# Row maxima sent from ScalarE's queue in an attention and mixture-of-experts kernel

## The chip, the cores and the metric

The kernel runs on one core of a Trainium2 chip. The metric is the time of one execution on the device in microseconds. The core has five engines with an instruction stream each: TensorE (PE, with its weight loads shown as PEld), VectorE (DVE), ScalarE (ACT), GpSimd (POOL) and SyncE (SP), which here does nothing but start transfers. Transfers between memories are done by 16 DMA engines that all streams share; an instruction in some engine's stream starts ("issues") them.

## The reference

The inputs are q, k and v of shape (8, 8, 1152, 64) and the weights of a small mixture of experts. What is computed:

```python
q_pool = q.reshape(B, H, S // 2, 2, D).mean(axis=3)          # 576 queries
scores = scale * np.matmul(q_pool, k.transpose(0, 1, 3, 2))
scores = scores - np.max(scores, axis=-1, keepdims=True)
attn = np.exp(scores)
attn = attn / (np.sum(attn, axis=-1, keepdims=True) + 1e-09)
out = np.matmul(attn, v)
x = out.transpose(0, 2, 1, 3).reshape(B * S, H * D)           # 4608 tokens of 512
e_idx = np.argmax(x @ w_gate, axis=1)                         # one of 8 experts
h = np.maximum(x[mask] @ w1[e], 0.0)
ye = h @ w2[e]
out[mask] = gate_w[mask, None] * eom[mask, e, None] * ye
```

The softmax subtracts the row maximum of the scores before the exponential. That maximum is what this case is about.

## The kernel before

**Tiling.** Attention goes over 32 pairs of heads (`pairs`: 8 batches, 4 pairs each). For a pair the 576 queries of each of two heads are multiplied with 1,152 keys in 9 blocks of 128 keys. One block of one head is a **step**; a pair has 18 steps and attention 576, written out by one Python loop (lines 566 to 593, `s` is the step). Numbers are kept accurate by splitting each fp32 operand into a rounded part and a remainder.

**A step** issues, in this order on the engines' streams: what was put off from the step before (`pendv`, lines 571 and 572), one piece of routing work for finished batches (`routers`), the score matmuls of this step (`scores`, four matmuls at lines 307 and 309 and two exponentials on ACT at lines 313, 314, 321 or 322, then a subtraction on DVE or POOL), preparation of later pairs (`prep_at`), one or two products for row maxima (`mgen`, lines 253 and 254), in some steps a transpose of maxima (`rows`), and in even steps the value matmuls of a step six earlier (`av`, lines 336 to 338). The scores use two PSUM buffers (`sps`) in turn, so the matmuls of a step wait until the exponentials of two steps earlier have read theirs.

**Row maxima.** The scores are computed twice. About one pair ahead, `mgen` multiplies queries by keys for the maxima alone: 27 products a pair (two or three matmuls each), each reduced by DVE (line 254) into a column of `pm`. They come in two groups: the first 15 products are query tiles 0 to 4, the next 12 tiles 5 to 8. After a group DVE reduces `pm` to `m9` (line 261), and the group is put into `pend_t`. `rows` (line 277), called in every step, transposes it on PE one step later at the earliest (line 282, a matmul with the identity), so that each query's maximum lies along a row. `split` (lines 286 to 291) turns the row into two parts, `mr`, on DVE, and sends them by two transfers into rows 66 and 67 of `qb`, from where the second pair of score matmuls (line 309) subtracts them. `split` runs at once in the first 18 steps, and later through `pendv`, at the head of the next step. The first group of a pair must have landed by the pair's first step, the second by its tenth.

**Queues.** All plain transfers are issued by SP, in program order: `dmaf` (line 119) for the copies of K and Q parts into `ka`, `kb`, `qa` and `qb` (`dk`, `dq`, `dl`) and for `mr`; `lk` and `lv` load K, Q and V. An instruction waits at the head of its stream, and all behind it wait too.

**PSUM.** Products for maxima, transposes, routing and the matmul for V's scale share three banks (`banks`). `psum(True)` holds a bank until `free`; the others are used in turn, the one that was freed longest ago first.

**V's scale.** Per pair ACT takes the sums of |V| (`amax`), PE adds them over partitions (`gmax`, line 195), and three small operations (`scale` 0, 1 and 2: DVE, POOL, DVE) make a power-of-two scale `sc`, which ACT uses in `vh`. The tables `PREP0` (first two pairs) and `PREP` (the others) say when each piece of preparation is issued, in thirds of a step: an entry (r, name) with r larger by 3 comes a step later, and r modulo 3 picks the place in the step (for pairs from 5 on: 0 behind the scores, 1 behind the first product, 2 at the end).

After attention come the experts (`Moe.run`), which this change does not touch.

## Time and profile before

| What | us |
|---|---|
| median of 3 runs | 1597.64 (1593.31 to 1597.94) |
| profiled execution, its own time | 1605.6 |
| its span, first to last instruction | 1603.8 |
| TensorE busy | 1531.7 |
| ScalarE busy | 1086.7 |
| VectorE busy | 1082.6 |
| GpSimd busy | 994.6 |
| first and last score step (start of line 307) | 33.1 and 1055.8 |
| mean granted TensorE clock | 0.98 of full speed |

The durations in the text are from the profiled execution. Busy time of TensorE counts pipelined matmuls whose ends are modelled, so that waits of less than about 0.15 us between two of them hide inside it; the starts in the timeline show those. Transfers issued by SP are not counted as busy time of any engine; their rows have the time that the issue itself took, not that of the data. In rows of waits, the numbers are the total in us, the number of waits and the longest. In rows of the timeline, the first two numbers are the start and the duration in us, and square brackets at the end hold the idle time before the instruction and what ended it. In rows of windows stand the stretch, its length, the busy time and count of instructions of each engine, the granted TensorE clock, the share of time that the DMA engines are busy, and GB/s.

### The profile page before, as it was taken

Reading aid. Unit: us, or ns where it says so; the run is one execution under the profiler, and the core shown is the slowest. Engines: PE = TensorE matmul, PEld = TensorE weight load, DVE = VectorE, ACT = ScalarE, POOL = GpSimd, SP = SyncE. Lnnn points to the kernel's source line nnn. Section 1 sums busy time; section 2 is a strip of 40 time slices with the busy share of each in tenths; the row PEclk is TensorE's granted clock in tenths of the full one; section 3 lists DMA queues with packets and bytes.
Section 4 is the critical chain, followed back from the end, with each engine's and each line's share of the span. In section 5 each row is a group of like instructions: output and inputs, shape, how many; then the busy total and the mean of one; then the engine's idle time right before and its main releaser. Section 6 shows DMA issues by size and latency. Waiting matters only on the chain. (4 is left out here: it accounts for less than half of the span.)

```text
span 1603.8 us, 42290 instructions
## 1 busy us (share of the span) xinstructions
PE 1531.7 (96%) x16618; PEld 1413.5 (88%) x16618; DVE 1082.6 (68%) x2222; ACT 1086.7 (68%) x1862; POOL 994.6 (62%) x917
## 2 busy tenths in 40 slices
PE   4999999999999999999999999879999999999996
PEld 3899999998998989899899999868999999999996
DVE  4577777776777777677677777666566666656662
ACT  2678888887888888788888888844444544544451
POOL 4778788878789789689878988634222232323200
PEclk9799999999999999999999999979999999999999
DMA  7756655675466466546666564247455645363500
GB/s 208 206 127 160 161 143 131 169 178 129 124 171 168 128 154 167 144 127 151 164 149 157 154 172 122 89 170 263 132 173 197 197 151 198 125 208 105 203 22 26
DMA packets 88756, 245.50 MB, mean 153 GB/s; under 512 B 13082, under 2 KB 17370, under 8 KB 88546
## 3 DMA queue, kind: packets, MB, share of 16 engines
q1 hardware_dynamic: 78826, 221.07, 49.7%
q0 software_dynamic: 9728, 21.67, 4.3%
q8 instruction: 135, 2.21, 0.6%
q14 instruction: 67, 0.55, 0.1%
HBM read 165.04 MB, written 23.81 MB: 118 GB/s over the span
## 5 line engine op out<-in xcount | busy, mean ns | idle before, releaser
L254 DVE TENSOR_REDUCE pm<-mp 128x1 f32<-128x384 f32 x864 | 456.8, 551 | 254.3 <-PE mp L253 248.9
L323 POOL TENSOR_TENSOR pl<-p,ph 128x576 f16<-128x576 f32 x381 | 488.1, 1286 | 176.6 <-ACT ph L322 153.7
L253 PE MATMUL mp<-ka,qa 128*128 128x384 f32 x960 | 319.2, 349 | 20.6 <-DMA qa<-yq 18.6
L321 ACT ACTIVATE p<-sps 128x576 f32<-128x576 f32 x381 | 249.0, 654 | 113.4 <-PE sps L309 104.2
L336 PEld LDWEIGHTS <-ph 128*128 128x128 f16 x2880 | 263.8, 97 | 42.9 <-issue 33.2
L336 PE MATMUL av<-vt,ph 128*128 128x65 f16 x2880 | 299.0, 195 | 0.0
L337 PE MATMUL av<-vt,ph 128*128 128x64 f16 x2880 | 296.5, 195 | 0.0
L338 PE MATMUL av<-vt,pl 128*128 128x65 f16 x2880 | 295.6, 193 | 0.0
L307 PE MATMUL sps<-qa,ka 128*128 128x288 f32 x1152 | 282.7, 327 | 6.4 <-DVE pl L317 6.3
L337 PEld LDWEIGHTS <-ph 128*128 128x128 f16 x2880 | 267.4, 98 | 0.4
L338 PEld LDWEIGHTS <-pl 128*128 128x128 f16 x2880 | 267.5, 99 | 0.0
L309 PE MATMUL sps<-qb,kb 68*128 68x288 f32 x1152 | 251.7, 301 | 14.8 <-DMA qb<-mr 14.8
L253 PE MATMUL mp<-kb,qb 66*128 66x384 f32 x768 | 264.3, 344 | 0.6 <-DMA kb<-kp 0.6
L322 ACT ACTIVATE ph<-sps 128x576 f16<-128x576 f32 x381 | 247.4, 649 | 0.0
L309 PEld LDWEIGHTS sps<-qb,kb 68*128 68x128 f32 x1152 | 189.3, 193 | 16.5 <-DMA qb<-mr 16.5
L253 PEld LDWEIGHTS mp<-ka,qa 128*128 128x128 f32 x960 | 182.0, 194 | 23.5 <-issue 18.9
L795 ACT ACTIVATE hh<-hps 128x512 fp32r<-128x512 f32 x88 | 52.6, 597 | 221.3 <-PE hps L792 221.3
L792 PE MATMUL hps<-xh,w1h 128*128 128x256 f32 x704 | 200.4, 285 | 0.0
L792 PE MATMUL hps<-xl,w1h 128*128 128x256 f32 x704 | 200.3, 284 | 0.0
L792 PE MATMUL hps<-xh,w1l 128*128 128x256 f32 x704 | 199.6, 283 | 0.0
L307 PEld LDWEIGHTS sps<-qa,ka 128*128 128x128 f32 x1152 | 185.6, 193 | 10.4 <-DVE pl L317 7.0
L313 ACT ACTIVATE ph<-sps 128x576 f16<-128x576 f32 x195 | 127.6, 654 | 58.5 <-PE sps L309 51.0
(170 smaller groups left out, 3190.0 us busy)
## 6 DMA issues: line engine op xcount, KB each, us to landing
ka<-xk SPq DMA_DIRECT2D x128, 288.0 KB
raw1b<-in_w_dram SPq DMA_DIRECT2D x24, 1024.0 KB
raw2b<-in_w_dram SPq DMA_DIRECT2D x24, 1024.0 KB
raw1a<-in_w_dram SPq DMA_DIRECT2D x22, 1024.0 KB
raw2a<-in_w_dram SPq DMA_DIRECT2D x22, 1024.0 KB
qp<-in_qT_dram SPq DMA_DIRECT2D x32, 576.0 KB
kpf<-in_kT_dram SPq DMA_DIRECT2D x32, 576.0 KB
vp<-in_vL_dram SPq DMA_DIRECT2D x32, 576.0 KB
```

Source lines behind the costliest of these rows:

```text
L253: nc.tensor.matmul(mp, lhsT=l, rhs=r, start=j == 0, stop=j == len(ops) - 1)
L254: nc.vector.tensor_reduce(out=pm[:, i:i + 1], in_=mp, axis=AX.X, op=ALU.max)
L307: nc.tensor.matmul(sps[:, j, 0:288], lhsT=ka[:, h, ks], rhs=qa[:, o + 288 * j:o + 288 * j + 288], start=True, stop=False)
L309: nc.tensor.matmul(sps[:, j, 0:288], lhsT=kb[:, h, ks], rhs=qb[:, h, 288 * j:288 * j + 288], start=False, stop=True)
L313: nc.scalar.activation(out=ph2, in_=x, func=AF.Exp, scale=1.0 / 16)
L321: nc.scalar.activation(out=p32.rearrange("p (j n) -> p j n", j=2), in_=x, func=AF.Exp, scale=1.0 / 16)
L322: nc.scalar.activation(out=ph2, in_=x, func=AF.Exp, scale=1.0 / 16)
L323: nc.gpsimd.tensor_tensor(out=pl, in0=p32, in1=ph, op=ALU.subtract)
L336: nc.tensor.matmul(av_[:, qb, 0:65], lhsT=hi, rhs=vt[:, h, c, 0:65], start=c == 0 and qb == 0, stop=False)
L337: nc.tensor.matmul(av_[:, qb, 0:64], lhsT=hi, rhs=vt[:, h, c, 66:130], start=False, stop=False)
L338: nc.tensor.matmul(av_[:, qb, 0:65], lhsT=lo, rhs=vt[:, h, c, 0:65], start=False, stop=c == NC - 1 and qb == 4)
L792: nc.tensor.matmul(hp[:, f], lhsT=W1[w][:, c, fs], rhs=d[x][:, c], start=i == 0, stop=i == 11)
```

## The change

Three edits in attention:

- The two transfers of `mr` are issued from ACT's queue instead of SP's. They are no longer issued by `split` itself; `split` puts them on a list (`pendd`), and `sends` issues them at the head of a later step, ahead of all other work of that step on ACT.
- From step 18 on, `rows` is called in even steps only. A transpose that was due in an odd step comes one step later; that concerns the second group of a pair nearly always, the first group in a few early pairs.
- In `PREP`, `gmax` moves by two thirds of a step (for pairs from 5 on: from an odd step, between two products, to the next step, an even one with one product, behind the scores), and `scale` 0 and 1 by a third.

```diff
-        (63, 'lv'), ..., (91, 'gmax'), (93, 'scale', 0), (94, 'scale', 1), (99, 'scale', 2), ...
+        (63, 'lv'), ..., (93, 'gmax'), (94, 'scale', 0), (95, 'scale', 1), (99, 'scale', 2), ...
...
-        def dmaf(o, i):
-            nc.sync.dma_start(out=o.bitcast(F32), in_=i.bitcast(F32))
+        def dmaf(o, i, q=nc.sync):
+            q.dma_start(out=o.bitcast(F32), in_=i.bitcast(F32))
...
-        pend_t = []
+        pend_t, pendd = [], []
+
+        def sends():
+
+            while pendd and pendd[0][1] < now[0]:
+                pendd.pop(0)[0]()
+
...
                     free(tk)
-                    for j in range(2):
-                        dmaf(qbf[66 + j:67 + j, 128 * t0:128 * t1].rearrange("o (t n) -> o t n", n=128), mr[:, j])
+
+                    def send():
+                        for j in range(2):
+                            dmaf(qbf[66 + j:67 + j, 128 * t0:128 * t1].rearrange("o (t n) -> o t n", n=128), mr[:, j], nc.scalar)
+                    pendd.append((send, now[0]))
...
                 if s >= -int(L0):
                     adv('m', mg, int(1.5 * (s + 1 + L0)))
                     now[0] = s
+                    sends()
                     pop(3)
                     rows()
             for s in range(18 * NP + 14):
...
+                sends()
                 while pendv:
                     pendv.pop(0)()
...
                 adv('m', mg, mw)
-                rows()
+                if s < 18 or s % 2 == 0:
+                    rows()
```

## The prediction

> **What bounds the kernel now.** I began with the page: span and busy times, then the waits of TensorE, longest first.

> ```profile
> span 1603.8 us, 42290 instructions
> PE 1531.7 (96%) x16618; PEld 1413.5 (88%) x16618; DVE 1082.6 (68%) x2222; ACT 1086.7 (68%) x1862; POOL 994.6 (62%) x917
> PE sps L309 <- DMA qb<-mr: 14.8, 8, 3.0
> PE tp L282 <- DVE pm L254: 2.1, 7, 0.3
> ```

> TensorE (PE) has work for 96% of the span and every other engine for two thirds, so a change counts for what it takes out of, or puts into, TensorE's stream. Its dearest wait inside attention is the one that this change touches: 14.8 us in 8 waits, by the second pair of score matmuls (L309) for the row maxima (`mr`). Next, how large these waits are at the start, and how the transfers are issued.

> ```profile
> PE sps L309 <- DMA qb<-mr: 5.9, 2, 3.0
> L120 SPq DMA_DIRECT2D qb<-mr x128: 579/683/1109, 33.7 to 1029.4; - x128
> ```

> The first row is the same list up to 150 us: pairs 0 and 1 have 5.9 us of the 14.8, so 8.9 us lie in pairs 7 and later. The second row: 128 issues from SP, 683 ns each in the middle, 1,109 at most. Why do they come late? The timelines of SP, VectorE and TensorE around one wait (first score step of pair 11) tell.

> ```profile
> 374.78 3.96 SPq L120 DMA_DIRECT2D ka<-xk  x4
> ...
> 385.05 0.46 SPq L120 DMA_DIRECT2D kb<-kp  x1
> 385.75 1.57 SPq L120 DMA_DIRECT2D qb<-mr  x2
> 381.22 0.28 DVE L288 SCALAR_TENSOR_TENSOR mr<-tp,mr 5x128 fp32r<-5x128 f32 x1
> 389.32 0.43 PE L307 MATMUL sps<-qa,ka 128*128 128x288 f32 x2
> 391.60 0.82 PE L309 MATMUL sps<-qb,kb 68*128 68x288 f32 x2 [1.85 <-DMA qb<-mr]
> 392.21 0.52 PE L253 MATMUL mp<-ka,qa 128*128 128x384 f32 x1
> ```

> The maxima are ready at 381.50, but SP is in a chain of issues for a later pair's K and Q, about 1 us each at first, and comes to them at 385.75: 4.25 us lost. Their two issues end at 387.32, the data count as landed at 391.60; TensorE was out of work from 389.75 (391.60 - 1.85). And L253 now takes 0.52 us, where it takes 0.34 otherwise. So I asked for windows with the granted clock: five stretches of half clock, and two for the DMA load around this wait.

> ```profile
> 36.26:46.50 10.24, 9.96 (x36) 9.48 (x37) 5.45 (x11) 6.51 (x11) 5.70 (x5) 0.50 0.73 209
> 70.39:80.63 10.24, 9.84 (x83) 9.26 (x84) 2.97 (x6) 3.58 (x6) 4.38 (x5) 0.50 0.43 150
> 391.24:398.07 6.83, 6.47 (x47) 6.00 (x48) 2.03 (x4) 3.05 (x5) 4.63 (x5) 0.50 0.05 19
> 647.24:654.07 6.83, 6.73 (x48) 6.26 (x49) 2.29 (x5) 3.05 (x5) 3.65 (x4) 0.50 0.07 9
> 776.95:780.36 3.41, 3.41 (x38) 3.41 (x36) 0.56 (x1) 2.26 (x5) 2.90 (x4) 0.50 0.06 19
> 382.00:389.00 7.00, 6.92 (x81) 6.26 (x80) 5.72 (x14) 5.59 (x10) 5.41 (x8) 1.00 1.04 232
> 392.00:398.00 6.00, 6.00 (x47) 5.50 (x47) 1.96 (x4) 3.05 (x5) 3.87 (x4) 0.50 0.01 4
> ```

> The third column from the right is the clock. Each stretch of 0.50 begins within a microsecond of the end of one of these waits (pairs 0, 1, 11, 19, 23). **A wait is paid twice**: as idle time, and as half speed behind it. [...]

> **The change, part by part.** Steps are counted from a pair's first score step, which needs its first group of maxima; the second group is needed nine steps later.

> *Issue from ScalarE (ACT).* The first group's split stays where it is (step -5; here it ends at 381.50) and its two issues go into ACT's stream at the head of step -4, behind the exponentials of step -5. What ACT does there, then the same place for the second group (head of step +4, pair 12), each with the TensorE row that needs the score buffer of that step again:

> ```profile
> 382.62 0.65 ACT L314 ACTIVATE sps<-sps 128x576 f32<-128x576 f32 x1
> 384.16 0.65 ACT L321 ACTIVATE p<-sps 128x576 f32<-128x576 f32 x1 [0.89 <-PE sps L309]
> 384.70 0.64 ACT L322 ACTIVATE ph<-sps 128x576 f16<-128x576 f32 x1
> 385.67 0.65 ACT L313 ACTIVATE ph<-sps 128x576 f16<-128x576 f32 x1 [0.32 <-PE sps L309]
> 386.12 0.43 PE L307 MATMUL sps<-qa,ka 128*128 128x288 f32 x2
> 432.46 0.65 ACT L322 ACTIVATE ph<-sps 128x576 f16<-128x576 f32 x1
> 434.31 0.65 ACT L321 ACTIVATE p<-sps 128x576 f32<-128x576 f32 x1 [1.20 <-PE sps L309]
> 434.86 0.65 ACT L322 ACTIVATE ph<-sps 128x576 f16<-128x576 f32 x1
> 436.56 0.50 PE L307 MATMUL sps<-qa,ka 128*128 128x288 f32 x2
> ```

> In step -4 ACT is idle 0.89 us before its exponentials, which end at 385.34, and their buffer is wanted at 386.12: 0.89 + 0.78 = 1.67 us of room. In step +4: 1.20 + (436.56 - 435.51) = 2.25 us. The trace has no issue on ACT. The nearest row is the same transfer on SP, 1.57 us for two here; the ends are 0 (wholly beside the activation that runs) and 2 x 1.109 = 2.22 us. I take 1.57, starting after the last exponential ends: it fits both places. Behind the two issues stand the next exponentials, and for those TensorE waits two steps later and VectorE or GpSimd (`pl`) in the same step; the delay of 0.68 us (1.57 - 0.89) is worked off in the gaps of the next steps (0.32 in step -3). For what is not, I take 2 us in all (0 to 17: at 2.22 us, 0.55 x 31 pairs). The wait that ACT gains, for the split, costs nothing from pair 2 on, since the split is over before the exponentials of its own step end.

> The second issue then ends at about 383.27 + 1.57 = 384.84. With the landing time seen here (391.60 - 387.32 = 4.28 us) it lands at 389.12, before TensorE runs out of work at 389.75. So **all six waits from pair 7 on go: 8.9 us**, and with them 6.83 + 6.83 + 3.41 = 17.07 us at half clock, worth half: **8.5 us**. Without the four-microsecond queue on SP, what is late next? K and Q of the next pair: TensorE's list has no such wait after pair 0, and SP loses 128 issues of 683 ns, so they come earlier.

> Pairs 0 and 1 have 5.9 us of waits and 20.48 us at half clock (10.2 us). In pair 0:

> ```profile
> 33.71 1.60 SPq L120 DMA_DIRECT2D qb<-mr  x2
> 30.90 0.28 DVE L288 SCALAR_TENSOR_TENSOR mr<-tp,mr 5x128 fp32r<-5x128 f32 x1
> 33.09 0.43 PE L307 MATMUL sps<-qa,ka 128*128 128x288 f32 x2
> 36.54 0.85 PE L309 MATMUL sps<-qb,kb 68*128 68x288 f32 x2 [3.03 <-DMA qb<-mr]
> ```

> Split over at 31.18, two issues to 32.78, landing 1.23 us later as now (36.54 - 35.31): 34.0, where TensorE is out of work from 33.51 (36.54 - 3.03), so some 0.5 us stay of 3.03. The other engines are not far behind TensorE there, and in pair 1 ACT would wait for a split of its own step. Of 16.1 us I take **10** (4 to 15).

> *Second transposes one step later.* Only the second group of a pair moves, from step +1 (behind two products of maxima) to step +2 (behind one, ahead of the value matmuls), where the first group already stands in its own step:

> ```profile
> 329.84 0.34 PE L253 MATMUL mp<-kb,qb 66*128 66x384 f32 x1
> 330.48 0.27 PE L282 MATMUL tp<-ident,m 128*4 128x128 f32 x1 [0.30 <-DVE pm L254]
> 317.07 0.33 PE L253 MATMUL mp<-kb,qb 66*128 66x384 f32 x1
> 317.24 0.27 PE L282 MATMUL tp<-ident,m 128*5 128x128 f32 x1
> 319.35 0.43 PE L253 MATMUL mp<-ka,qa 128*128 128x384 f32 x1
> 319.62 0.34 PE L253 MATMUL mp<-kb,qb 66*128 66x384 f32 x1
> ```

> From start to start 0.64 us in the second group, 0.17 in the first: 0.47 saved in each of the 7 waits of the list's row, **3.3 us** (0 to 4). Split and issue go a step later too; of five steps to step +9 none is needed.

> *The matmul for V's scale* moves from step -5 to -4, its follow-ups by a third of a step; the last (reciprocal, step -2) stays, and so does ACT's use of it. Beside it in step -5 the next product takes 0.27 us from start to start (last two rows above) where 0.18 is usual; in 32 pairs that is 2.9 us, but the loading of weights may cost it at any place. **1 us** (0 to 3).

> Sum: 8.9 + 8.5 + 10 + 3.3 + 1 - 2 = 29.7 us, on the profiled execution's 1605.6 us: 1575.9. That execution stands 8.0 above the median of the runs, 1597.64. If the lost time makes up that difference the median falls by 21.7, if not by 29.7. I take the middle: **1572 us**.

> **Rivals.**

> *ACT's issues cost more than the room* (faster, but less). At 1,109 ns each the loss is 17 us instead of 2: 29.7 - 15 = 14.7, about 1587 us. If half clock has another cause than these waits and stays, 8.5 and some 6 of the 10 are lost, 15 us remain and the time is the same. [...] For dear issues: the gap in step -3 is only 0.32 us. Against them: the row of this very place, 1.57 us. Against another cause of the slow clock: five stretches, each at such a wait.

> *The maxima still land late* (no change). The DMA engines are full when they are issued (share 1.04) and empty after the landing (0.01): if the landing waits for that backlog to drain and not for SP's queue, waits and half clock stay, and 3.3 + 1 - 2 = 2.3 us remain: 1595 us. Against: pair 0's landing in 1.23 us at a share of 0.73.

> *ACT waits for SP's descriptor work* (slower). In steps -5 to -3 SP issues without a pause. If two queues cannot issue at once, each ACT issue waits for one of SP's, 0.46 to 0.99 us by the rows above, say 0.73: the two take 1.57 + 1.46 = 3.03, which is 1.36 over the room, x 31 pairs = 42 us, against 31.7 gained: 10 us slower, 1612 with the same 4 us off. It decides from 1.67 + 31.7/31 = 2.7 us for two issues. [...]

> **How the numbers follow.** Chances: forecast 0.65, expensive issues (with half clock that stays) 0.13, late landing 0.11, lock 0.11. A measurement of this kernel can tell about 0.3% from no change, 4.8 us here. The first two are faster by more (0.78), the third is within it, the fourth slower. The forecast's own range goes from 1558 (pairs 0 and 1 give 15, transposes and V's scale 7, ACT costs 0, nothing of the 8.0 us is lost time) to 1586 (4, 0, 2, all of it is); to 1591 it takes in the second case: 0.78.

> **What would show it.** Right: the wait of L309 for `mr` falls from 14.8 us to below 2, clock 1.00 from 85 us to the end of attention, L282 without a wait for `pm`, issues of `qb<-mr` on ACT right after the split. Wrong: L307 waiting for ACT or VectorE in steps -2 and -1 of most pairs (dear issues); issues on ACT well over 0.7 us while SP is busy (lock); early issues with L309 still waiting (landing).

## The result, and the profile after

The kernel after takes **1580.92 us** (median of 4 runs, 1574.08 to 1584.72), the kernel before 1597.79 (4 runs beside them): a ratio of 0.989, 95% interval 0.9845 to 0.9934. Forecast were 1572 us and a range of 1558 to 1591. The profiled execution took 1584.72 us, its span is 1583.0.

The line numbers have moved: the transpose is now L288 (was L282), the split L293 and L294, the score matmuls L316 and L318 (were L307 and L309), the exponentials L322, L323, L330 and L331, `pl` on VectorE L326. First the span and busy times of the page, and TensorE's waits, longest first (total in us, number, longest):

```profile
span 1583.0 us, 42321 instructions
PE 1514.3 (96%) x16618; PEld 1408.7 (89%) x16618; DVE 1077.6 (68%) x2222; ACT 1086.1 (69%) x1862; POOL 994.0 (63%) x917
...
PE sps L316 <- DVE pl L326: 8.8, 7, 4.5
PE sps L316 <- ACT ph L331: 6.8, 8, 1.6
PE sps L318 <- DMA qb<-mr: 4.7, 2, 2.4
```

The wait for the maxima fell from 14.8 us to 4.7, and the transpose's wait for `pm` is gone. In their place stands a row that the list of before doesn't have: 6.8 us behind ACT's exponentials (L331). Then the issues, in the groups by tile, and the stretches of half clock that lie inside attention before pair 31, with two clear ones between them, in windows:

```profile
L120 ACTq DMA_DIRECT2D qb<-mr x128: 587/669/1287, 31.8 to 1009.3; - x128
```

```profile
35.75:42.58 6.83, 5.74 (x21) 5.49 (x22) 2.74 (x5) 3.98 (x7) 3.21 (x3) 0.50 0.90 223
85.00:100.00 15.00, 13.37 (x168) 12.11 (x166) 11.04 (x28) 11.22 (x23) 11.00 (x11) 1.00 1.00 225
100.60:107.43 6.83, 6.11 (x46) 5.83 (x47) 1.66 (x5) 3.05 (x5) 3.31 (x4) 0.50 0.00 1
110.00:250.00 140.00, 138.64 (x1875) 131.01 (x1873) 104.49 (x255) 118.03 (x221) 118.42 (x105) 1.00 0.58 150
257.62:261.03 3.41, 3.41 (x38) 3.10 (x37) 1.28 (x3) 2.17 (x4) 2.74 (x4) 0.50 1.02 239
506.79:510.20 3.41, 3.32 (x34) 3.01 (x35) 1.39 (x3) 2.98 (x6) 2.19 (x3) 0.50 0.97 250
```

An issue takes 669 ns on ACT in the middle, where it took 683 on SP. The half clock in pairs 1, 11, 19 and 23 is gone; three stretches are new, in pairs 2, 6 and 14 (100.60, 257.62 and 506.79). In pair 31 there is one of 6.83 us (at 1018.79), where the kernel before has one of 3.41 (at 1043.19).

Where the time went shows when the start of a pair's first score matmul is subtracted from that of the next pair's (timeline of TensorE; us, sums over the pairs named):

| stretch | before | after | difference | forecast |
|---|---|---|---|---|
| to the first score matmul | 33.1 | 34.0 | +0.9 | |
| pairs 0 and 1 | 73.8 | 64.6 | -9.2 | -10 |
| pair 2 | 31.7 | 36.4 | +4.8 | 0 |
| pairs 7, 11, 15, 19, 23 | 169.8 | 151.4 | -18.3 | -17.4 |
| pairs 6, 10, 14, 18, 22, 26 | 184.4 | 193.5 | +9.1 | up to +2 |
| pair 31, without its last step | 28.9 | 32.1 | +3.2 | 0 |
| the other 17 pairs | 534.2 | 525.6 | -8.5 | -4.3 for all pairs |
| from the last score step to the end | 548.0 | 545.3 | -2.7 | 0 |

So the waits went as forecast, the ordinary pairs gained well over the forecast, and 17 us were given back in three places (9.1 + 4.8 + 3.2). The last row is no effect of the change that can be told from chance: in the runs below, whose experts are the same, that stretch takes between 545.1 and 552.9 us. The experiments are about the rest: which edit brings what, and what the three places are.

**The pairs 6, 10, 14, ...** In the timelines of SP, ACT and TensorE in pair 6, at the sends of pair 7's first group:

```profile
244.38 3.90 SPq L120 DMA_DIRECT2D ka<-xk  x4
...
252.93 0.60 SPq L120 DMA_DIRECT2D kb<-kp  x1
```

```profile
251.72 0.65 ACT L322 ACTIVATE ph<-sps 128x576 f16<-128x576 f32 x1
252.27 0.65 ACT L323 ACTIVATE sps<-sps 128x576 f32<-128x576 f32 x1
253.74 1.96 ACTq L120 DMA_DIRECT2D qb<-mr  x2
255.75 0.65 ACT L330 ACTIVATE p<-sps 128x576 f32<-128x576 f32 x1 [2.84 <-PE mp L253]
```

```profile
257.00 0.53 PE L316 MATMUL sps<-qa,ka 128*128 128x288 f32 x2 [1.41 <-ACT ph L331]
257.36 0.46 PE L318 MATMUL sps<-qb,kb 68*128 68x288 f32 x2
257.62 0.51 PE L253 MATMUL mp<-ka,qa 128*128 128x384 f32 x1
```

In an ordinary pair the first issue begins 0.15 us behind the start of the first exponential, beside the running ones; here it begins 0.82 us after the last has ended, and the next exponential stands behind it. TensorE waits 1.41 us, and 3.41 us of half clock follow (257.62).

**Pair 2.** The rule "even steps only" moves the transpose of its first group from step 31 to step 32; the split ends at 94.48, the issues follow, the data are used at 101.32 and TensorE waits 2.32 us (the second wait of the row for `mr`).

**Pair 31.** The cast of the experts' first weights (L773) stands two steps earlier in ACT's stream than before, where its data have not come yet:

```profile
1017.21 1.05 ACT L773 CAST w1h<-raw1a 128x1024 fp32r<-128x1024 f32 x1 [3.49 <-DMA raw1a<-in_w_dram]
```

TensorE loses 4.51 us behind it, by way of the late exponentials and their `pl`: the longest of the 8.8 us above.

### The profile page after: what moved, and what is told of

The parts are those of the page before. It is cut to its first block, busy times and chain, and to the rows that moved or that the text cites. A ratio compares the mean times of both kernels' runs of the same rounds, so it can differ in the third digit from the quotient of the medians.

```text
span 1583.0 us, 42321 instructions
## 1 busy us (share of the span) xinstructions
PE 1514.3 (96%) x16618; PEld 1408.7 (89%) x16618; DVE 1077.6 (68%) x2222; ACT 1086.1 (69%) x1862; POOL 994.0 (63%) x917
## 5 line engine op out<-in xcount | busy, mean ns | idle before, releaser
L254 DVE TENSOR_REDUCE pm<-mp 128x1 f32<-128x384 f32 x864 | 453.7, 550 | 228.8 <-PE mp L253 224.5
L253 PE MATMUL mp<-ka,qa 128*128 128x384 f32 x960 | 317.3, 347 | 21.2 <-DMA qa<-yq 20.1
L330 ACT ACTIVATE p<-sps 128x576 f32<-128x576 f32 x381 | 249.1, 654 | 101.9 <-PE sps L318 61.8
L345 PEld LDWEIGHTS <-ph 128*128 128x128 f16 x2880 | 263.6, 97 | 39.9 <-issue 30.7
L345 PE MATMUL av<-vt,ph 128*128 128x65 f16 x2880 | 297.3, 194 | 0.0
L316 PE MATMUL sps<-qa,ka 128*128 128x288 f32 x1152 | 279.6, 324 | 15.8 <-DVE pl L326 8.8
L253 PE MATMUL mp<-kb,qb 66*128 66x384 f32 x768 | 262.4, 342 | 0.8 <-DMA kb<-kp 0.8
L318 PE MATMUL sps<-qb,kb 68*128 68x288 f32 x1152 | 249.2, 299 | 4.7 <-DMA qb<-mr 4.7
L331 ACT ACTIVATE ph<-sps 128x576 f16<-128x576 f32 x381 | 247.7, 650 | 0.0
L316 PEld LDWEIGHTS sps<-qa,ka 128*128 128x128 f32 x1152 | 185.4, 192 | 20.9 <-DVE pl L326 9.3
L253 PEld LDWEIGHTS mp<-ka,qa 128*128 128x128 f32 x960 | 179.9, 191 | 24.4 <-issue 20.3
L318 PEld LDWEIGHTS sps<-qb,kb 68*128 68x128 f32 x1152 | 187.9, 192 | 5.1 <-issue 5.1
L326 DVE TENSOR_TENSOR pl<-sps,ph 128x576 f16<-128x576 f32 x195 | 146.6, 752 | 26.9 <-ACT sps L323 23.5
```

Of the source, the lines that this page charges most:

```text
L253: nc.tensor.matmul(mp, lhsT=l, rhs=r, start=j == 0, stop=j == len(ops) - 1)
L254: nc.vector.tensor_reduce(out=pm[:, i:i + 1], in_=mp, axis=AX.X, op=ALU.max)
L316: nc.tensor.matmul(sps[:, j, 0:288], lhsT=ka[:, h, ks], rhs=qa[:, o + 288 * j:o + 288 * j + 288], start=True, stop=False)
L318: nc.tensor.matmul(sps[:, j, 0:288], lhsT=kb[:, h, ks], rhs=qb[:, h, 288 * j:288 * j + 288], start=False, stop=True)
L326: nc.vector.tensor_tensor(out=pl.rearrange("p (j n) -> p j n", j=2), in0=x, in1=ph2, op=ALU.subtract)
L330: nc.scalar.activation(out=p32.rearrange("p (j n) -> p j n", j=2), in_=x, func=AF.Exp, scale=1.0 / 16)
```

## The experiments

Ratios are against the kernel before, run on the same chip beside them (medians of 1598.5 to 1599.1 us).

### The edits one by one

**e1, the queue alone**: the kernel after with the old table and `rows` in every step.

```diff
-                if s < 18 or s % 2 == 0:
-                    rows()
+                rows()
...
-        ..., (93, 'gmax'), (94, 'scale', 0), (95, 'scale', 1), ...
+        ..., (91, 'gmax'), (93, 'scale', 0), (94, 'scale', 1), ...
```

> The changed kernel with the transposes in every step and V's scale in its old step: only the queue is changed. Theory A (my reading of the two traces: the queue edit removes the late maxima and the half clock behind them, but loses some 11 us where ACT's issues meet SP's in the pair before every fourth one; the step edits bring about 11 us and cost 5 in pair 2): 1581 + 11 - 5 = about 1587 us, no wait of the score matmuls for the maxima in pair 2, no stretch of half clock at 100 us. Rival B (the queue edit brings all, the step edits nothing but the wait in pair 2): about 1576 us.

1590.90 us, ratio 0.995 (0.9931 to 0.9968): 7.6 us, some 4 short of theory A; rival B falls. In stretches as in the table, the pairs 7, 11, 15, 19 and 23 gain 17.2 us and the pairs 0 and 1 8.9; the pairs 6, 10, 14, ... lose 9.3 (4.6 of them in pair 26 alone, where half clock follows a wait for `xb`) and pair 31 3.2. Pair 2 takes 31.6 us, as before.

**e2, the two step edits alone**: the kernel before with the even steps and the new table; SP still issues the maxima.

```diff
-                rows()
+                if s < 18 or s % 2 == 0:
+                    rows()
...
-        ..., (91, 'gmax'), (93, 'scale', 0), (94, 'scale', 1), ...
+        ..., (93, 'gmax'), (94, 'scale', 0), (95, 'scale', 1), ...
```

> The kernel before with the even-step rule for the transposes and the new place of V's scale, transfers still issued by SP. Theory A: the eight or nine waits for the maxima stay, with half clock behind them, and 11 us come from the steps, of which pair 2 may take up to 5 back: 1587 to 1592 us. Rival B: no gain, 1598 us or more.

1583.54 us, ratio 0.9908 (0.9882 to 0.9933), below the range of theory A.

**e3, the new table alone**: the second half of that diff.

> The kernel before with V's scale in its new place, nothing else. Theory A (steps 13 and 14 of a pair are 0.34 us shorter after the change and step 16 0.1 longer, in 27 pairs): 6 to 7 us less, about 1591 us, with the same eight waits for the maxima. Rival: the prediction's own 1 us, about 1597, the shortening of steps 13 and 14 coming from the other edits.

1590.93 us, ratio 0.9961 (0.9946 to 0.9976).

The wait of L309 for `mr` in e2 and in e3:

```profile
PE sps L309 <- DMA qb<-mr: 15.0, 7, 3.7
```

```profile
PE sps L309 <- DMA qb<-mr: 14.1, 9, 3.2
```

The waits for the maxima stay whole in both, and yet e2 is 15 us faster than before and e3 7.6. So most of the gain of the change does not come out of the waits it is aimed at: the two small edits alone nearly reach the time of the whole, and the queue, which brings 7.6 us alone (e1), adds 2.6 us to them (1583.54 to 1580.92, intervals that overlap). The parts don't add up (7.6 + 15.0 against 17 for the whole), in the traces mainly because pair 2 loses its 4.8 us only where the later transposes and the queue come together: it takes 31.6 us in e1, 31.4 in e2 and 36.4 after. The even steps alone are the difference of e3 and e2, 7.4 us in the medians, with intervals that nearly meet, and 6.4 in the profiled executions, of which 5.0 lie in step 1 of the pairs.

Why does one moved matmul bring 7 us? Here are the steps in question in the timeline of TensorE in pair 12, the kernel before and then e3:

```profile
448.32 0.28 PE L195 MATMUL tp<-am,onesf 128*128 128x2 f32 x2
448.46 0.43 PE L253 MATMUL mp<-ka,qa 128*128 128x384 f32 x1
448.73 0.34 PE L253 MATMUL mp<-kb,qb 66*128 66x384 f32 x1
449.13 0.42 PE L408 MATMUL tp<-xh,wgt 128*128 128x320 f32 x1
449.38 0.31 PE L408 MATMUL tp<-xl,wgt 128*128 128x320 f32 x1
449.54 0.43 PE L307 MATMUL sps<-qa,ka 128*128 128x288 f32 x2
```

```profile
442.21 0.34 PE L253 MATMUL mp<-ka,qa 128*128 128x384 f32 x1
442.39 0.34 PE L253 MATMUL mp<-kb,qb 66*128 66x384 f32 x1
442.57 0.31 PE L408 MATMUL tp<-xh,wgt 128*128 128x320 f32 x1
442.71 0.31 PE L408 MATMUL tp<-xl,wgt 128*128 128x320 f32 x1
442.86 0.42 PE L307 MATMUL sps<-qa,ka 128*128 128x288 f32 x2
...
443.39 0.28 PE L195 MATMUL tp<-am,onesf 128*128 128x2 f32 x2
443.53 0.42 PE L253 MATMUL mp<-ka,qa 128*128 128x384 f32 x1
443.78 0.33 PE L253 MATMUL mp<-kb,qb 66*128 66x384 f32 x1
```

The product behind L195 still takes 0.25 us from start to start where 0.18 is usual, as the prediction thought it might. What it did not look at stands two rows further: the routing matmul L408 started 0.40 us after that product and its second half 0.25 after the first; now it is 0.18 and 0.14. What held it shows in the waits of TensorE's weight loads, in the kernel before and in e3:

```profile
PEld tp L408 <- DVE pm L254: 11.2, 28, 0.6
```

```profile
PEld tp L408 <- DVE pm L254: 0.6, 1, 0.6
```

The matmul for V's scale holds one of the three banks until `scale` 0 frees it. Between the two products of an odd step that left two banks, and the routing matmul had to wait until DVE had reduced a product (L254) and so emptied its bank. In e1, where the matmul stands in its old place, the row is again 11.2 us in 28 waits. The two steps together go from 3.54 us to 3.18, and a later one gives back 0.1 in three pairs of four; over all pairs steps 13 to 17 take 7.7 us less in e3's profiled execution (7.6 in the median).

### The three places

**e4, pair 2**: the kernel after, with the even steps from pair 2 on.

```diff
-                if s < 18 or s % 2 == 0:
+                if s < 36 or s % 2 == 0:
```

> The changed kernel with the even-step rule from step 36 on instead of 18, so that the first transpose of pair 2 stays in step 31. Theory A: the wait of 2.4 us in pair 2 goes, and with it the half clock at 100 us (6.83 us): 5 us less than the changed kernel, about 1576 us. Rival: the wait comes from the landing of the data under load and not from the later step; it stays, about 1581 us.

1579.94 us, ratio 0.9888 (0.9868 to 0.9907). The wait for `mr` is now that of pair 0 alone, pair 2 takes 31.3 us, and the windows show the clock:

```profile
34.70:44.94 10.24, 9.52 (x35) 9.07 (x36) 5.04 (x10) 6.16 (x11) 5.69 (x5) 0.50 0.78 220
45.00:1010.00 965.00, 950.01 (x12873) 894.93 (x12871) 709.14 (x1759) 811.08 (x1497) 816.64 (x731) 1.00 0.60 153
```

From 45 us to the last pair it is 1.00 throughout. The mechanism holds. The median gained 1 us instead of 5, though, within the intervals; this execution has 10.24 us of half clock in pair 0 where the one of after had 6.83.

**e7, pair 31**: e4, with the last pair's transfers on SP.

```diff
-                            dmaf(..., mr[:, j], nc.scalar)
+                            dmaf(..., mr[:, j], nc.sync if now[0] >= 18 * NP - 26 else nc.scalar)
```

> As e4 (1579.9 us), but the two groups of the last pair go over SP's queue as before, so that the cast of the experts' first weights stands behind two more steps of exponentials in ACT's stream. Theory A: the wait of 3.5 us for that weight's load in front of the last pair's exponentials, and TensorE's 4.5 us behind it, go back to about 1: 1576.5 us, last pair's steps 28 to 29 us instead of 32. Rival B: the experts' part then starts later by the same time and nothing is gained: 1580.

1576.97 us, ratio 0.9863 (0.9844 to 0.9882). Pair 31 takes 28.0 us (31.8 in e4), and the cast in front of it waits 0.58 us instead of 3.49. As theory A had it; but the intervals of e4 and e7, 3.0 us apart in the medians, overlap.

**e8, one transfer a step**: e7, the first transfer at the head of step -4, the second one step later.

```diff
-                    def send():
-                        for j in range(2):
-                            dmaf(...)
-                    pendd.append((send, now[0]))
+                    def send(j):
+                        dmaf(...)
+                    for j in range(2):
+                        pendd.append((functools.partial(send, j), now[0] + j))
```

> As e7, and the two transfers of a group are issued one a step (heads of steps -4 and -3, +4 and +5). Theory A (what the change still loses is ACT and SP holding each other up, about 11 us in pairs 6, 8, 10, 14, 18, 22, 26): each block is half as long and fits into the room of its step, the waits of L316 behind ACT fall from 6.8 us to below 3, TensorE's steps there lose 5 to 6 us less: about 1571. Rival B (the second transfer now lands late): waits of L318 for mr of 1 us or more come back in pairs 7, 11, 15, 19, 23, and the time is 1577 or more.

1574.59 us, ratio 0.9843 (0.9828 to 0.9857). It tells little: the waits behind `ph` are gone from TensorE's list, but 4.0 us behind `sc` (L205) and 3 more waits for `mr` have come, and the pairs 6, 10, 14, ... gain 1.5 us in all six. The intervals of e7 and e8, 2.4 us apart in the medians, overlap.

**e9, a step later there**: e7, with the first groups of the pairs 3, 7, 11, ... sent one step later.

```diff
-                    pendd.append((send, now[0]))
+                    pendd.append((send, now[0] + (now[0] % 72 == 49)))
```

> As e7, and in the pairs 3, 7, 11, ... the first group's two transfers go one step later (head of step -3), past the end of SP's long chain of issues. Theory A (the loss in pairs 6, 10, 14, 18, 22, 26 is the collision of the two queues): ACT's issues there take 0.65 us each and start behind the running exponential, those pairs' steps 15 lose no 1.3 to 1.8 us, 8 us less in all: about 1568.5. Rival B: landing too late at step 0, waits for mr of 1 us or more in those pairs: 1577 or more. Rival C (step 15 loses its time to something else, as the reduction on GpSimd and VectorE): no change, 1576.5.

1572.35 us, ratio 0.9826 (0.981 to 0.9842): the fastest of all. But not by theory A, and where the 4.6 us to e7 lie stays open: the profiled execution of e9 (1575.56 us) is the slowest of its five and that of e7 (1571.78) the fastest of its four, so the two traces don't show the gain. In the timeline of ACT in pair 6, SP issues nothing from 247.57 to 248.44, and still ACT's second issue is late:

```profile
246.21 0.72 ACTq L120 DMA_DIRECT2D qb<-mr  x1
246.70 0.64 ACT L331 ACTIVATE ph<-sps 128x576 f16<-128x576 f32 x1
247.91 0.69 ACTq L120 DMA_DIRECT2D qb<-mr  x1
248.69 0.65 ACT L322 ACTIVATE ph<-sps 128x576 f16<-128x576 f32 x1 [1.35 <-PE mp L253]
```

ACT does nothing from 247.34 to 247.91, and step 16 loses 0.8 us there (2.76 us in the median of those pairs, 1.91 elsewhere) where in e7 step 15 lost as much. So something else than two queues that issue at once holds ACT up. The records of the trace name it. Each of the 726 transfers that SP and ACT issue has one of eight numbers in its record, 90 or 91 transfers each in before and in after: that of a **completion semaphore**, a counter whose increments the trace shows as the data land. In before, where SP issues them all, the eight come in turn without an exception; in after they go in the order of the program over both queues. In front of 125 of ACT's 128 issues in after stands a wait for the issue's own number, and so for the landing of the eighth transfer before. Here, in e9, that is a part of Q that SP issued at 241.14; its last increment came at 247.83, and 0.08 us later ACT issues. In pair 6 of the kernel after the two are parts of K that SP issued at 245.54 and 246.64 and that landed at 253.67 and 254.94; the issues begin at 253.74 and 255.02. In five runs (after, e4, e7, e8, e9) 57 of ACT's 568 issues for the pairs from 3 on began over 0.2 us after the end of what stood before them in ACT's stream. Each of the 57 began 0.08 us behind the landing of the eighth transfer before it; 35 of them are those for the pairs 3, 7, 11, ....

**e12, the test of that**: e7, and in every fourth pair four transfers of 64 bytes more in SP's chain, whose data nobody reads. What they change for ACT is whose landing it has to wait for.

```diff
                 dmaf(qb[0:64, h], xq[r])
+                if h == 1 and n % 4 == 0 and n > 1:
+                    for j in range(4):
+                        extra = sm.tile([1, 16], F32R, name="extra%d" % j, bufs=1)
+                        dmaf(extra, xq[64:65, 0:16])
```

> As e7 (1577.0 us), and in every fourth pair, in the SP chain that lies in front of the sends of the pairs 3, 7, 11, ..., four small transfers of 64 bytes more, behind those of xq, into a buffer that nobody reads. Theory A (an issue takes the completion semaphore of the eighth transfer before it, on SP or ACT, and waits until that one has landed): the four shift this by one to two transfers; ACT's issues there now wait for a later transfer of the chain, start within 0.1 us behind its landing, 0.7 to 1.5 us later than in e7, and the pairs 6, 10, 14, ... lose 1 to 2 us more each: 1584 to 1590. Theory B (the two queues only hinder each other while both issue): the four are over before ACT's issues begin, nothing more is lost: 1577 to 1579. Theory C (SP's longer chain makes K and Q late): L253 waits for ka, kb, qa or qb.

1588.84 us, ratio 0.9933 (0.9909 to 0.9958): 12 us slower than e7, inside theory A's range; the pairs 6, 10, ... 26 take 15 us more, 2.5 each, half clock included, where 1 to 2 were expected. The products for maxima have no new wait for K or Q, so theory C falls. The timelines of SP and ACT in pair 6:

```profile
242.97 1.29 SPq L120 DMA_DIRECT2D qb<-xq  x1
...
245.60 2.98 SPq L120 DMA_DIRECT2D extra<-xq  x4
```

```profile
246.27 3.21 ACTq L120 DMA_DIRECT2D qb<-mr  x2
249.53 0.65 ACT L334 ACTIVATE p<-sps 128x576 f32<-128x576 f32 x1 [3.18 <-DMA qb<-mr]
```

ACT's second issue begins at 248.79 (inside the row of two); the `qb` part that SP issued at 242.97, eight transfers earlier, landed at 248.72. The same in four other pairs (375.17 after 375.09, 502.25 after 502.17, 628.70 after 628.62, 754.77 after 754.70). The two queues themselves hardly hindered each other: ACT's first issue (246.27 to 246.98) and one of SP's (246.25 to 246.83) ran side by side in 0.71 and 0.58 us. Over seven runs (after, e1, e4, e7, e8, e9, e12; pairs from 3 on), the first transfer of a first group took 701 ns on ACT in the median both in 95 cases that overlapped an issue of SP by more than 0.2 us and in 71 that overlapped none; the second took 687 ns in 104 and in 19. A few that overlapped took longer, up to 1.25 us.

**e13, other semaphores**: e7, with these first groups issued from GpSimd, whose transfers carry another eight (in before and in after 172 of them, with eight other numbers in turn).

```diff
-                            dmaf(..., nc.sync if now[0] >= 18 * NP - 26 else nc.scalar)
+                            dmaf(..., nc.sync if now[0] >= 18 * NP - 26 else nc.gpsimd if now[0] % 72 == 50 else nc.scalar)
```

> As e7 (1577.0 us), but the first groups of the pairs 3, 7, 11, ... 27 are issued from GpSimd's queue, which has completion semaphores of its own. Theory A (what is lost there is ACT's wait for the landing of SP's transfers): the 1.0 to 1.8 us in step 15 of the pairs 6, 10, 14, ... go, 1.3 us x 6 or 7 = 8 to 9 us: 1568. Theory B (the block only moves: GpSimd's two issues, about 1.05 us each by its other issues, hold up its pl): L316 or L345 waits for pl, 1 to 2 us in the same pairs: 1575 to 1580. Theory C (from GpSimd the data lands late): L318 waits for mr: 1580 and more.

1592.62 us, ratio 0.9963 (0.994 to 0.9987). ACT's loss goes entirely (step 15 of those pairs takes 1.33 us, 2.15 in e7), as theory A said, and theory C takes the gain and more. The waits of TensorE, and GpSimd's timeline:

```profile
PE sps L318 <- DMA qb<-mr: 13.3, 7, 4.1
```

```profile
246.38 2.53 POOL L332 TENSOR_TENSOR pl<-p,ph 128x576 f16<-128x576 f32 x2
248.85 1.10 POOL L120 DMA_DIRECT2D qb<-mr  x2
```

The issues are short, 0.55 us each, but they stand behind two `pl` and begin at 248.85, 4.35 us before the first step wants the data (253.20); in e7 ACT's first begins 6.90 us before. They landed at 254.01 and 255.30.

### What an issue on ACT costs

**e5, every transfer twice**, to the same rows. The edit was made to the kernel after itself, not to e4.

```diff
-                        for j in range(2):
+                        for j in (0, 1, 0, 1):
```

> The kernel after with the later transposes from step 36 on (e4, 1579.9 us), and every transfer of the maxima issued twice from ACT, with the same data: 128 more issues of about 0.67 us, 86 us of ACT. It prices an issue on ACT. Theory A (ordinary pairs have room for two issues and not for four): four take 2.7 us, about 0.5 of it beside the activation that runs, 2.2 are left against 1.67 us of room in step -4 and 2.25 in step +4, so 0.5 us in each of 32 pairs = 16 us, and the seven places where ACT and SP issue at the same time lose twice as much, 11 us more: about 1607 us. Rival B (issues cost only where SP issues too): 11 us, 1591. Rival C (each issue is on the path everywhere): 86 us, 1666.

1826.72 us, ratio 1.1438 (1.138 to 1.1497), beyond every theory. The timeline of ACT says that the experiment priced something else:

```profile
327.23 0.71 ACTq L120 DMA_DIRECT2D qb<-mr  x1
327.63 0.65 ACT L323 ACTIVATE sps<-sps 128x576 f32<-128x576 f32 x1
328.04 4.33 ACTq L120 DMA_DIRECT2D qb<-mr  x3
332.42 0.65 ACT L330 ACTIVATE p<-sps 128x576 f32<-128x576 f32 x1 [4.14 <-DMA qb<-mr]
```

The third issue writes what the first one writes, so it waits for that landing: in 63 of 64 groups it begins 0.02 us behind it (at most 0.08). In this group ACT does nothing for 4.14 us; over a group's issues it is idle for 4.0 us in the median of the 64, where it is 0.5 in the kernel after. Together with the half clock behind (mean clock 0.923) the whole costs 3.8 us a group (246 us over the kernel after, in 64 groups).

**e10, twice without a wait**: e7, with the copies going to a buffer of their own.

```diff
+                        if now[0] >= 36 and now[0] < 18 * NP - 26:
+                            dup = sm.tile([2, 5, 128], F32R, name="dup", bufs=1)
+                            for j in range(2):
+                                dmaf(dup[j:j + 1, 0:nt], mr[:, j], nc.scalar)
```

> As e7 (1577.0 us), and behind each group's two transfers two more of the same data from ACT's queue, into a buffer of their own that nobody reads, in pairs 2 to 30: 58 groups, 116 issues of 0.66 us, 77 us of ACT. In e5 the copies went to the same rows and ACT waited for the first transfer's landing in front of the third issue; here nothing has to be waited for. Theory A (an ordinary step has room): four issues take 2.7 us from the first exponential's start, 1.5 to 1.65 us beyond the end of the exponentials, inside the room of 1.67 and 2.25 us, so only the places where SP issues too lose more, 6 to 9 us: 1583 to 1586 us. Theory B (half of the room is used up already by the two issues there are): 0.3 to 0.5 us in each group and those places, 1603 to 1615. Theory C (what ACT issues is on the path): 77 us or more, 1654.

1633.89 us, ratio 1.0233 (1.02 to 1.0267): 57 us for 114 issues, above the range of theory B. Where they are lost: medians over the pairs from 4 to 29 of the time of a step show that the second group's place (step 4 and behind) loses next to nothing, 2.26 us as in e7 and 0.1 us in step 6. Nearly all of what attention loses, 50 of 54 us in the profiled executions, is in the first group's (steps 15 to 17 of the pair before): 1.28 us more in step 15 of the pairs 5, 9, ..., 1.40 in 7, 11, ..., 0.6 in 4, 8, ..., and about 4 in the three steps of 6, 10, .... Two more issues last 1.2 to 1.4 us. In the pairs 5, 9 and 17, for example, the four follow one another with at most 0.25 us between them, so there the two of the change have used up the room; in 6, 10, ... the issues also wait for landings, up to 1.8 us. In the second place there is room for four.

**e11, ACT only where SP is late**: e9, with 11 of the 64 groups on ACT and the other 53 on SP (the expectation counted 52).

```diff
+                    act = now[0] < 26 or now[0] % 72 == 49 and now[0] < 18 * NP - 26
...
-                            dmaf(..., nc.sync if now[0] >= 18 * NP - 26 else nc.scalar)
-                    pendd.append((send, now[0] + (now[0] % 72 == 49)))
+                            dmaf(..., nc.scalar if act else nc.sync)
+                    if act:
+                        pendd.append((send, now[0] + (now[0] % 72 == 49)))
+                    else:
+                        send()
```

> As e9 (1572.4 us), but ACT issues only pairs 0 and 1 and the first groups of the pairs 3, 7, 11, ... 27, where SP's chain was in the way before; all other groups, 52 of 64, go over SP again, straight behind their split. Theory A (an issue on ACT costs nothing in an ordinary pair): the same within 2 us, 1572. Theory B (each ordinary group costs about 0.1 us on ACT): 5 us less, 1567. Theory C (on SP some of the 52 land late, or SP's other loads do): waits of L318 for mr or of L253 for K and Q come back, 1576 or more.

1576.99 us, ratio 0.9866 (0.9844 to 0.9888). The pairs 4, 8, 12, ... take 30.76 us in both, so the issues on ACT cost them nothing. The 4.6 us that e11 is slower lie in step 16 of the pairs 5, 9, 13, ... (2.69 us, 1.91 in e9), where an exponential on ACT waits 1.30 us for a signal of TensorE (at 345.36). It isn't any of the three theories, and its cause stays open.

## Why the prediction was right, and where not

The time, 8.9 us above the forecast, lay in the range, and the direction was right; the attribution was right for the waits at which the change is aimed and wrong for most of the rest. Point by point:

- **Six waits from pair 7 on, 8.9 us, and the half clock behind them, 8.5.** Right. The five pairs with the waits of over 1 us fall by 18.3 us, of which 1.2 (five times 0.24) belong to V's scale: 17.1 against 17.4. In pair 11 the data land at 385.18 and are used at 386.30, where 0.6 us were forecast between.
- **Half clock comes from the waits.** Right: every stretch of it between 45 us and pair 31, in after and in all experiments but e5 (whose waits stand too close for it), begins behind or in a wait of TensorE of 1.41 us or more (in e9 behind two in a row), and e4, e7, e8 and e11 have none at all there. The rival "half clock has another cause" falls. In pair 6 a wait of 1.41 us was enough for 3.41 us of half clock. But not every such wait had its price: 1.57 us in e2 and 1.70 in e4 had no half clock behind them; both lie across an edge of the grid of 3.413 us on which the records of the clock begin (last section). So 8.5 us was this one execution's price: e2, with 8.1 us of waits in the pairs 7, 11, 15, 19 and 23, has 10.2 us of half clock behind them instead of 17.07.
- **Pairs 0 and 1, 10 us.** Right in size (9.2). But the edit that would give it back was not looked at: of "the first group in a few early pairs" that comes a step later, pair 2's was one, and 4.8 us went there. The step that failed is "Only the second group of a pair moves".
- **ACT's issues, 2 us (0 to 17).** The price was right: 669 ns measured for 683, and nothing lost in the ordinary pairs (the pairs 4, 8, ... take the same time in e9 and e11), where the room of 1.67 us was the right one to compare it with; e10 shows that little or none of it was left. The step that failed is "The wait that ACT gains, for the split, costs nothing": the split was not the only thing an issue waits for. In front of it stands the wait for the landing of the eighth transfer before, and at the sends of the pairs 7, 11, 15, ... that was a part of K or Q under way for 8 us (245.54 to 253.67 in pair 6, 371.34 to 379.50 in pair 10). That cost 9.1 us net, and some 10.6 without the 1.5 (six times 0.25) that V's scale brings in the same pairs; e2, where ACT issues nothing, takes 10.6 us less there.
- **Rival "ACT waits for SP's descriptor work"** (the lock of the chances). Its mechanism falls as a price of 0.73 us for each issue, by the two issues side by side in e12 (0.71 us on ACT, 0.58 on SP) and the equal medians with and without an overlap (701 ns for the first transfers, 687 for the second). Its place (the steps in which SP's chain runs) and the idea that ACT inherits SP's delays were the right ones. That two queues cannot issue at once is shown by no run; only a few overlapping issues took longer, up to 1.25 us, and why is open.
- **Rival "the maxima still land late".** Not in the kernel after, but what it says of a backlog shows in the rows. Behind parts of K and Q that were issued earlier and were still under way, the maxima took about as long from issue to landing from either queue: issued at 385.75 by SP before, landed at 391.46 with the second (5.71 us); issued at 379.58 by ACT after, landed at 385.18 (5.60), both for pair 11; issued at 245.56 by ACT in e7, landed at 251.41 (5.85), again with the second. From the end of its issue the second took 4.14 us before and 3.79 after in pair 11, where the ordinary pairs have 2.4 and 3.0 in the median. So in these rows the change gains by issuing earlier, and not by the queue. And e13 paid for issuing later: its waits are 13.3 us, 1.9 of them in pair 0.
- **Second transposes, 3.3 us.** Right: step 1 of the pairs 5, 9, ... goes from 1.87 us to 1.31, in seven pairs 3.9 us, and L288's wait for `pm` is gone. The even steps brought more than this wait (7.4 us by the medians of e3 and e2); the rest is not accounted for.
- **V's scale, 1 us (0 to 3).** Wrong by a factor of seven (7.6 measured in e3). The step that failed is that it asked for what stands right behind the moved matmul (0.27 for 0.18 us) and blamed the loading of weights, and not for the bank that the matmul holds: the routing's matmul two places behind waited for a bank and lost 0.33 us more. The row for that, 11.2 us in 28 waits, stood in the trace of before.
- **The last pair** was in no term: 3.2 us, because an instruction that waits (L773) came two steps earlier in ACT's stream.
- **What would show it.** The wait of L318 below 2 us: no, 4.7, of which pair 0 has 2.4 and pair 2 2.3. Clock 1.00 from 85 us to the end of attention: no, four stretches. L288's wait: gone. Issues right behind the split: yes, but for the pairs 6, 10, 14, .... L316 waiting for ACT in most pairs: no, in 8 places.

In the profiled executions the sum of 29.7 us stands against 20.9 measured (1605.6 to 1584.7); the median fell by 16.9, since the profiled execution of after too lies above its median, by 3.8. The terms that came out worse (7 us at ACT, 4.8 in pair 2, 3.2 in pair 31) and those that came out better (nearly 7 at V's scale, 2.7 behind attention) cancel in part, which is how a sum with wrong terms came out 9 us off. That the time lies inside the range is thus in part luck: without the unforeseen gain at V's scale the median would have been near the range's upper end.

## What to carry to other kernels

Before a transfer is moved to the queue of an engine that computes, ask not only how long its issue takes (669 ns here) but what it waits for. Here it shared eight completion semaphores with SP's transfers, so that in five runs 57 of ACT's 568 issues stood waiting until 0.08 us behind the landing of the eighth transfer before, and what stood behind them on ACT waited too: in pair 6 of the kernel after ACT ran no exponential for 2.84 us, of which the two issues themselves took 1.40, and TensorE waited 1.41. A place where the older one has landed is worth a trial: one step later brought 4.6 us in the median (e9), though the traces don't show where. And when an instruction is moved out of a crowded step, ask which buffer it held there, and look at all that follows in the step, not only at the next instruction.
